# A new order for the steps of a fused attention and expert-layer kernel, behind a fixed beginning

## The chip, the cores and the metric

The kernel runs on one core of one Trainium2 chip. The metric is device time in microseconds of one execution. The kernel before takes 298.82 us, the median of three runs (298.56 to 299.05).

## The reference

The first half is a causal attention with a decay per head and no softmax, over 8 batches of 8 heads, 576 positions and 64 channels; its result, regrouped by position, is the input x (4608 rows of 512) of the second half:

```
scores = scale * np.matmul(q, k.transpose(0, 1, 3, 2))
ret = scores * Dmat          # Dmat = gamma_h ** (i - j) for i >= j, else 0
x = np.matmul(ret, v) ...    # (4608, 512)
h = x @ w_in                 # (4608, 2048)
s = np.sin(alpha * h)
g = h + s * s / (alpha + 1e-09)
out = g @ w_out              # (4608, 512)
```

## The kernel before, in words

The whole work is a list of 1214 small steps, written one to a line in the string TABLE (L18 to L1233). `run` (L1975) splits a line into a name and words and calls the function of that name; nothing reorders the steps afterwards (`tc.manual_schedule()`). So the order of the lines is, engine by engine, the order of the instructions, and each engine takes its own in that order. What one engine needs of another it waits for by semaphore. Words with an @ name the buffer that the step writes (`@raw3`, `@ss1`): a buffer's next writer waits for its last reader. V, A and G name the engine: VectorE, ScalarE, GpSimd (POOL in the profile).

*Blocks.* x is cut into nine blocks of 512 rows. Block b (0 to 7) holds positions 0 to 511 of batch b; block 8 holds the last 64 positions of all eight batches. While TensorE works on the expert layer of block b, the attention of a later batch is made between its matmuls.

*The expert layer.* `project n fc tag` (L1737) is four 512-column matmuls, unit fc (of 16) of block n, into the PSUM bank `tag` (h0, h1, h2, op; m0 and m1 are pairs of banks). `sine` (L1750, ScalarE) reads the bank; `square` (L1758, any engine) squares the sine; `product` (L1767, VectorE) adds the bank to the scaled square and writes g. Only then is the bank free. For blocks 0 to 2, `gemm2 n u tag` (L1780) is four matmuls with w_out and `finish` (L1774) copies 128 finished rows and stores them. From block 3 on the last product is made with seven products of sub-matrices in place of eight: `weight_sum` and `row_sum` (L1814, L1824) make the sums, `part_product` (L1841) is 16 matmuls of 256 columns, and `after_product` (L1875) adds up and stores; `part_product n 7 - first=6` goes on in the bank of product 6, when `after_product n 6` has read it.

*The attention of batch b.* `load` (L1339) brings half p of q, k or v by SyncE's DMA queue into a `raw` buffer; `cast` (L1360) scales it to 16 bits. q and k are transposed on TensorE (`turn`, L1422, then `take`) for batches 0 and 1, later by DMA (`crossed`, L1415, on SyncE's queue too). `at.outer` (L1493) makes the sums of k times v of each 128 positions; `take_sum`, `evict` and `evict_bank` (L1523) copy them out of PSUM; `more` (L1548, two GpSimd instructions) and `next_sum` add them up; `to_state` (L1539) scales the running state. `at.scores` (L1554) and `at.masked` (L1572, VectorE) make the masked scores. `at.values` (L1584) multiplies them with v in two passes (False, then True), and `at.add_states` (L1617) adds the part of the earlier positions. `at.keep` (L1635) copies the result out of PSUM into x: with one engine in one copy, with two in two halves. The first `project` of block b needs both halves p of `at.keep b`. A run of attention matmuls between matmuls of the expert layer is called a stretch.

*Marks.* The second pass of `at.values` may only start when the first is done. With `relay=G` (batches 4 to 7) and in `ends.values` (block 8's attention, L1683) this goes by way of GpSimd: `told` (L1458) puts a no-op into GpSimd's queue that waits for the first pass, and the second pass waits for that no-op:

```
def told(last, eng):
    mark = eng.nop()
    order(mark, last)
    return mark
```

The no-op stands behind all that was put on GpSimd before it. `wait_for_w_out g` (L1918) is a tiny DMA on SyncE's queue that reads a quarter of w_out, so SyncE waits there until that quarter is loaded.

## Time and profile before

| | |
|---|---|
| median of three runs | 298.82 us |
| the profiled execution | 298.66 us |
| its span, first to last instruction | 296.9 us |
| mean granted TensorE clock | 0.989 |
| busy: TensorE, VectorE, ScalarE, GpSimd | 283.9, 234.5, 198.6, 172.6 us |
| `project`: 532 of its matmuls, mean | 372 ns each, overlapping |
| `product` on VectorE | 144 of 743 ns |
| `sine` on ScalarE | 144 of 683 ns |
| `square` on ScalarE, VectorE, GpSimd | 93 of 629, 30 of 510, 21 of 1042 ns |

Matmuls are pipelined, so their pace is read from the starts of two groups and not from the length of one. A row of the timeline gives the start, the length, the engine, the line of the code, the operation, what it writes and reads, and in brackets how long the engine sat idle before it and what ended that. A row of the chain gives start, length and engine with the tile and line. Idle time of an engine other than TensorE costs nothing by itself.

### The profile page before, as it was taken

The numbers are of one execution on the slowest core, as the hardware profiler recorded it, in microseconds if no ns is written. First come the engines' busy times: TensorE is split into PE (matmuls) and PEld (weight loads), VectorE is DVE, ScalarE is ACT, GpSimd is POOL, SyncE is SP. The second block draws the span as 40 slices with busy tenths as digits, with TensorE's granted clock in tenths as the row PEclk, the third lists the DMA queues.
The fourth block names the chain that finished last, engine by engine and source line by source line (L and its number), as shares of the span: only waits on it lengthen the run. The fifth ranks groups of instructions, "written<-read, shape, count | busy, mean of one in ns | idle before, by whom it ended". The sixth has DMA issues, their size and how long they took to land.

```text
span 296.9 us, 8432 instructions
## 1 busy us (share of the span) xinstructions
PE 283.9 (96%) x3480; PEld 182.8 (62%) x3480; DVE 234.5 (79%) x336; ACT 198.6 (67%) x323; POOL 172.6 (58%) x169
## 2 busy tenths in 40 slices
PE   5889999999899999999999999999999999999994
...
GB/s 217 349 230 210 254 293 326 211 196 308 261 237 172 244 171 182 153 253 175 161 240 189 192 140 192 123 199 138 79 55 106 72 4 38 71 0 39 35 107 107
DMA packets 121766, 49.95 MB, mean 168 GB/s; under 512 B 78720, under 2 KB 119680, under 8 KB 121728
## 3 DMA queue, kind: packets, MB, share of 16 engines
...
## 4 chain that ended last, share of the span: by engine, by line
PE 76%; DMA 9%; ACT 5%; DVE 3%; POOL 2%; SPq 2%; issue 2%; ACTq 0%
PE hps L1745 35%; PE hps L1849 23%; PE ops L1785 9%; DMA raw<-in_v_dram 5%; PE sc L1564 2%; PE o L1606 2%; DMA kT<-k 2%; DMA raw<-in_q_dram 2%; SPq L1418 1%; POOL k L1396 1%; ACT v L1320 1%; DVE gT L1769 1%; ACT s L1753 1%; PE kv L1506 1%; DVE xT L1322 1%
## 5 line engine op out<-in xcount | busy, mean ns | idle before, releaser
L1769 DVE SCALAR_TENSOR_TENSOR gT<-ss,inva,hps 128x512 f16<-128x512 f16 x144 | 104.5, 743 | 23.5 <-ACT ss L1762 16.1
L1753 ACT ACTIVATE s<-hps,alpha_t 128x512 f16<-128x512 f32 x144 | 95.8, 683 | 40.5 <-PE hps L1745 31.4
L1745 PE MATMUL hps<-xT,w_in 128*128 128x512 f16 (+1 forms) x532 | 119.3, 372 | 2.1 <-DVE xT L1322 0.9
L1745 PEld LDWEIGHTS <-w_in 128*128 128x128 f16 x596 | 66.1, 114 | 53.1 <-issue 1.6
L1762 ACT ACTIVATE ss<-s 128x512 f16<-128x512 f16 x93 | 58.2, 629 | 7.5 <-DVE gT L1769 5.2
L1764 POOL TENSOR_TENSOR ss<-s 128x512 f16<-128x512 f16 x21 | 21.8, 1042 | 46.7 <-ACT s L1753 34.4
L1785 PE MATMUL ops<-w_out,gT 128*128 128x512 f16 x192 | 45.4, 379 | 0.2 <-DVE gT L1769 0.2
L1396 POOL TENSOR_TENSOR k<-raw,cn 128x1024 f16<-128x1024 f32 (+1 forms) x16 | 26.7, 1676 | 29.3 <-DMA raw<-in_k_dram 29.2
L1849 PEld LDWEIGHTS <-gT 128*128 128x128 f16 x384 | 37.2, 98 | 8.5 <-issue 0.8
L1849 PEld LDWEIGHTS <-S 128*128 128x128 f16 x288 | 28.0, 98 | 5.7
L1785 PEld LDWEIGHTS <-gT 128*128 128x128 f16 x192 | 18.0, 98 | 21.1 <-issue 0.5
L1832 POOL TENSOR_TENSOR S<-gT,S 128x1024 f16<-128x1024 f16 x10 | 22.0, 2207 | 14.7 <-DVE S L1832 10.0
L1551 POOL TENSOR_TENSOR s<-kvs,cn 128x256 f32<-128x256 f32 x21 | 15.4, 735 | 14.0 <-ACT kvs L1320 10.0
L1849 PE MATMUL hps<-T,gT 128*128 128x256 f16 x192 | 22.9, 273 | 0.5 <-DVE mid L1880 0.5
L1764 DVE TENSOR_TENSOR ss<-s 128x512 f16<-128x512 f16 x30 | 15.3, 510 | 9.8 <-ACT s L1753 9.6
L1849 PE MATMUL hps<-w_out,gT 128*128 128x256 f16 x192 | 22.9, 273 | 0.0
L1849 PE MATMUL hps<-w_out,S 128*128 128x256 f16 x192 | 22.9, 273 | 0.0
L1576 DVE TENSOR_TENSOR ret<-sc,mask 128x1024 f16<-128x1024 f32 x16 | 19.2, 1219 | 4.2 <-PE sc L1564 4.2
L1552 POOL TENSOR_TENSOR kvs<-s,kvs 128x256 f32<-128x256 f32 x21 | 17.0, 811 | 2.4 <-DVE kvs L1322 0.9
L1320 ACT CAST xT<-o 128x1024 f16<-128x1024 f32 (+1 forms) x13 | 13.8, 1092 | 6.9 <-PE o L1628 5.2
L1396 POOL TENSOR_TENSOR q<-raw,cn 128x1024 f16<-128x1024 f32 x8 | 15.2, 1904 | 1.5 <-DMA raw<-in_q_dram 1.4
L1396 DVE TENSOR_TENSOR q<-raw,cn 128x1024 f16<-128x1024 f32 (+1 forms) x9 | 12.9, 1440 | 3.7 <-DMA raw<-in_q_dram 3.7
...
## 6 DMA issues: line engine op xcount, KB each, us to landing
...
```

The lines of the kernel that those rows point to most:

```text
L1320: eng.copy(d_, s_)
L1396: eng.tensor_tensor(dst[:, a0:a1].rearrange("p a r t d -> p t (a r) d"), t_.rearrange("p (t a) x -> p t a x", t=2)[:, :, a0:a1].rearrange( ...
L1552: nc.gpsimd.tensor_tensor(self.kvs[:, c], s32, self.kvs[:, c], ADD)
L1576: nc.vector.tensor_tensor(ret.rearrange("p t (z x) -> p (t z) x", z=2)[:, :, 0:n], sc.rearrange("p t (z x) -> p (t z) x", z=2)[:, :, 0:n], ...
L1745: matmul(hps_of[n, fc][0][:, cols], w_in16[fc // 4][:, a, fc % 4 :: 4], xs[n][:, a, cols], start=(a == 0 and part != 1), stop=(a == KT - 1 ...
L1753: nc.scalar.activation(s_t, hps, mybir.ActivationFunctionType.Sin, bias=0.0, scale=alpha_t[:, fc : fc + 1],)
L1762: nc.scalar.activation(ss_t, s_t, mybir.ActivationFunctionType.Square)
L1764: eng.tensor_tensor(ss_t, s_t, s_t, MULT)
L1769: nc.vector.scalar_tensor_tensor(gT[n][:, fc, :], ss_t, inva[:, fc : fc + 1], hps, MULT, ADD)
L1785: matmul(ops[n, c, cols.start][:, cols], gT[n][:, fk, c * P : (c + 1) * P], w_out16[:, fk, cols], start=(fk == 0), stop=(fk == FC - 1), sk ...
L1832: made = eng.tensor_tensor(out_, x, y, op)
L1849: matmul(acc[:, 256 * j : 256 * j + 256], lhs[:, x, 128 * j : 128 * j + 128], rhs[:, x], start=(tag is not None and j == js[0] and p == 0 ...
```

## The change

Only TABLE changes. The first 136 steps stay (up to `product 0 14`, about 33.4 us into the span); of the other 1078 steps, none is added or left out by name, but nearly all stand some places earlier or later, and many have other buffers or banks. 128 of them differ in an engine, a bank or a sub-step order as well:

| step | before | after |
|---|---|---|
| `square` on V, A, G | 30, 93, 21 | 27, 89, 28 |
| `row_sum` on V, G | 31, 17 | 27, 21 |
| `cast` of a whole tile on V, A, G | 11, 8, 36 | 7, 9, 39 |
| `at.evict_bank` on V, A | 6, 4 | 2, 8 |
| `at.take_sum` on V, A | 0, 5 | 2, 3 |

In batch 1, `at.scores 1 0 1` and `at.outer 1 (0)` stood apart and now stand together; in batch 2, `at.outer 2 (0,1)` and `at.scores 2 1 1` stood together and now stand apart. The number of stretches behind the fixed part is 25 in both.

The diff, cut to the places that are spoken of ("..." where lines are left out):

```diff
@@ -152,1083 +152,1083 @@
 at.scores 1 0 0 m1
 load 1 v 0 @raw3
 product 0 14
+load 1 k 1 @raw2
+product 0 10
 project 0 12 h1
 sine 0 12 @s2
-load 1 k 1 @raw4
-product 0 10
-load 1 v 1 @raw2
+square 0 12 A @ss2
+product 0 12
+load 1 v 1 @raw1
 project 0 13 h0
-sine 0 13 @s0
+cast 1 v 0 G @v163
+gemm2 0 4 op
+load 3 k 1 @raw4
 gemm2 0 12 h2
+load 2 k 0 @raw0
+gemm2 0 5 op
...
 at.masked 1 0 0 @ret0
-gemm2 0 4 op
-square 0 13 A @ss3
 at.scores 1 0 1 m0
-square 0 12 G @ss0
...
-cast 1 v 0 A @v162
-gemm2 0 5 op
...
+at.outer 1 (0) h0 h1
...
+at.take_sum 1 1 V @kvs0
+at.take_sum 1 0 V
...
+cast 1 k 1 V @k163
 gemm2 0 13 h2
...
 gemm2 0 14 h2
...
-at.outer 1 (0) h0 h1
-at.take_sum 1 1 A @kvs0
-at.take_sum 1 0 A
...
-cast 1 v 1 A @v161
...
-gemm2 0 6 op
...
-cast 1 k 1 V @k161
...
 gemm2 0 15 h2
...
+cast 1 v 1 A @v160
...
-load 2 q 0 @raw2
+gemm2 0 7 op
+finish 0 3
+wait_for_w_out 1
...
-gemm2 0 7 op
-at.masked 1 1 1 @ret2
...
+gemm2 0 0 h0
 at.masked 1 1 0 @ret3
...
-at.next_sum 1 3
-cast 2 k 0 G @k162
-gemm2 0 0 h0
-load 2 k 1 @raw1
-finish 0 3
-cast 2 q 0 G @q162
-load 2 v 0 @raw5
-gemm2 0 1 h0
-gemm2 0 2 h0
 at.values 1 0 False m1
 at.values 1 0 True
...
+at.add_states 1 0
...
-cast 2 q 1 V @q160
-at.add_states 1 0
-wait_for_w_out 1
...
-at.keep 1 0 V @xT2
+load 2 q 0 @raw3
+at.masked 1 1 1 @ret2
 at.values 1 1 False m0
+at.next_sum 1 3
+at.keep 1 0 V @xT1
 at.values 1 1 True
 at.add_states 1 1
+cast 3 k 1 G @k160
+finish 0 1
+cast 2 k 0 G @k163
+gemm2 0 1 h0
...
 at.keep 1 1 A
-gemm2 0 3 h0
-finish 0 0
-finish 0 1
-project 1 6 m0
...
-load 2 v 1 @raw3
+load 2 k 1 @raw4
+gemm2 0 2 h0
+project 1 6 m1
+load 2 v 0 @raw1
+cast 2 q 0 G @q160
+crossed 2 0 k @kT2
...
+load 2 v 1 @raw0
+cast 2 k 1 G @k162
+cast 2 q 1 V @q162
...
+crossed 2 1 q @qT3
 project 1 8 op
...
-cast 3 k 1 G @k160
...
+gemm2 0 3 h0
+cast 2 v 0 G @v161
...
-cast 2 k 1 G @k161
...
-crossed 2 1 q @qT2
-crossed 2 1 k @kT3
...
-cast 2 v 0 G @v161
...
+cast 2 v 1 G @v160
...
+crossed 2 1 k @kT3
...
-load 3 v 0 @raw2
...
+crossed 2 0 q @qT2
...
+at.outer 2 (0,1) m1
+load 3 k 0 @raw3
...
-cast 2 v 1 G @v160
-at.outer 2 (0,1) m1
...
+gemm2 0 8 h0
...
-crossed 2 0 q @qT3
-crossed 2 0 k @kT1
...
+gemm2 0 9 h0
...
 at.scores 2 1 1 m0
-load 3 k 0 @raw0
...
-gemm2 0 8 h0
-gemm2 0 9 h0
...
-load 3 v 1 @raw3
...
+load 3 v 1 @raw5
...
+load 3 v 0 @raw4
+gemm2 0 10 h0
...
-load 3 q 0 @raw4
...
-at.scores 2 0 0 m0
...
-gemm2 0 10 h0
...
+at.scores 2 0 0 m0
...
 at.add_states 2 0
 at.add_states 2 1
+cast 3 v 0 G (0) @v162
+cast 3 v 0 G (1)
+cast 3 k 0 G @k162
 at.outer 3 (0,1) op h2
-cast 4 v 0 G @v160
+at.keep 2 0 V A @xT0
+at.keep 2 1 A V
+gemm2 1 6 h0
+load 4 v 0 @raw5
+square 1 15 G @ss2
+product 1 15
+crossed 3 1 k @kT0
+at.evict_bank 3 1 A @kvs0
+project 2 7 m1
+at.evict_bank 3 0 A
...
+gemm2 1 12 h1
...
+gemm2 1 13 h1
...
+gemm2 1 7 h0
...
+gemm2 1 14 h1
...
+gemm2 1 15 h1
...
+gemm2 1 8 h0
...
-at.keep 2 0 V A @xT1
-at.evict_bank 3 1 A @kvs0
-at.evict_bank 3 0 V
...
-gemm2 1 6 h0
-gemm2 1 7 h0
-at.keep 2 1 A V
-project 2 7 m1
...
+project 2 14 h2
+at.evict_bank 4 0 A @kvs0
...
+project 2 8 op
 at.masked 3 0 1 @ret0
...
-project 2 14 h2
...
-at.masked 3 0 0 @ret2
-project 2 8 op
...
-at.evict_bank 4 0 V @kvs0
+at.values 3 0 False m0
+at.values 3 0 True
+at.add_states 3 0
 at.values 3 1 False m1
 at.values 3 1 True
...
+at.add_states 3 1
+at.keep 3 0 A V @xT2
+at.keep 3 1 A
...
+at.evict_bank 4 1 V
+product 2 14
+project 2 10 h0
...
+project 2 11 h1
...
+project 2 15 m1
...
-at.values 3 0 False m0
-at.values 3 0 True
-at.evict_bank 4 1 V
...
-at.add_states 3 0
...
-at.add_states 3 1
...
-at.keep 3 0 A V @xT0
...
-product 2 14
-at.keep 3 1 V
...
-project 2 10 h0
...
-project 2 11 h1
...
-project 2 5 h2
...
-project 2 12 m0
-project 2 15 m1
...
+row_sum 3 S4 1 G told_to=G
...
+cast 6 k 0 G @k161
...
+at.more 5 2 @s320
...
-cast 6 k 0 G @k161
...
 cast 6 q 0 G @q162
...
-row_sum 3 S4 1 V told_to=G
...
+at.to_state 5 1 G
...
+cast 6 v 1 G @v161
...
+at.to_state 5 2 G
...
+square 4 8 G @ss3
+at.more 5 3 @s320
 cast 6 k 1 G @k163
...
-at.to_state 5 0 @s160
...
-square 4 8 G @ss1
...
+row_sum 4 S3 0 G
...
+at.to_state 5 3
...
+at.values 5 0 False m0 relay=G
...
-at.to_state 5 3
-at.to_state 5 1 G
...
-at.to_state 5 2 G
...
-row_sum 4 S3 0 G
 at.values 5 1 False m1 relay=G
...
+square 5 6 G @ss3
...
-at.to_state 6 3
-row_sum 4 S4 1 G told_to=G
...
-square 5 6 A @ss0
...
-at.to_state 6 2
-cast 7 k 0 G @k161
+row_sum 4 S4 1 G told_to=G
...
-cast 7 k 1 G @k163
...
-row_sum 5 S3 0 G
...
 cast 4 k 2 G
...
+cast 7 k 1 G @k163
+cast 7 v 1 G @v163
...
+at.more 6 3 @s321
...
+at.to_state 6 0 @s161
...
+at.to_state 6 2
...
+cast 7 v 0 V @v162
...
+cast 2 q 2 G
...
+cast 7 q 1 G @q160
...
-cast 2 q 2 G
-cast 7 q 0 G @q160
...
+row_sum 5 S3 0 G
...
+at.to_state 6 1
+at.values 6 1 False m1 relay=G
...
 at.values 6 0 False m0 relay=G
-at.values 6 1 False m1 relay=G
...
-product 7 2
...
 ends.masked 0
...
+square 7 3 A @ss1
...
+product 7 3
+product 7 2
...
-square 7 3 V @ss1
-product 7 3
...
+ends.masked 2
...
-ends.masked 2
...
 part_product 6 6 op
...
+after_product 6 6
...
-after_product 6 6
...
+part_product 6 7 - first=6
...
-part_product 6 7 - first=6
...
-part_product 8 6 h0
...
+part_product 8 1 op
+row_sum 8 S2 0 G
+part_product 8 6 h2
...
+part_product 8 2 h0
...
+part_product 8 7 - first=6
...
+row_sum 8 S1 1 G
 row_sum 8 S4 1 V
...
-part_product 8 2 h1
-part_product 8 7 - first=6
-row_sum 8 S1 0 V
...
-row_sum 8 S1 1 G
-row_sum 8 S4 0 V
-part_product 8 5 op
...
+row_sum 8 S1 0 G
+part_product 8 5 h1
...
-part_product 8 4 m0
+part_product 8 4 m1
+row_sum 8 S4 0 G
+part_product 8 3 h1 (0)
...
-part_product 8 3 h2 (0)
+part_product 8 3 m0 (1)
...
-part_product 8 3 h1 (1)
```

More of the change, by code (lines that the diff above doesn't have):

```diff
@@ new lines @@
+project 2 15 m1
+sine 2 15 @s2
+product 2 11
+square 2 10 A @ss0
+product 2 10
+crossed 4 1 q @qT3
+project 2 5 h2
+sine 2 5 @s0
+project 2 12 m0
+sine 2 12 @s3
+square 2 12 G @ss1
+cast 0 k 2 G
+square 2 15 V @ss2
+load 5 q 1 @raw2
+square 2 5 V @ss0
+product 2 5
+gemm2 2 0 op
+project 3 1 h1
+load 1 q 2
+project 3 0 h0
+at.more 4 1 @s321
+at.to_state 4 1 G
+cast 5 v 0 A @v162
+product 2 12
+load 5 k 1 @raw5
+sine 3 1 @s2
+project 3 2 h2
+product 2 15
+sine 3 0 @s3
+square 3 0 A @ss3
+square 3 1 V @ss2
@@ new lines @@
+sine 3 10 @s3
+square 3 10 A @ss2
+project 3 8 h1
+crossed 0 2 k
+cast 5 k 0 G @k162
+at.masked 4 0 1 @ret2
+load 2 k 2
+project 3 12 m0
+project 3 11 h2
+load 2 q 2
+gemm2 2 8 op
+crossed 5 0 k @kT3
+gemm2 2 9 op
+sine 3 12 @s3
+gemm2 2 10 op
+gemm2 2 11 op
+crossed 5 1 k @kT2
+sine 3 11 @s2
+square 3 11 G @ss1
+product 3 10
+square 3 12 A @ss3
+product 3 12
+at.to_state 4 3 G
+at.to_state 4 2 A
+cast 5 v 1 A @v163
+product 3 11
+finish 2 2
+at.values 4 1 False m1 relay=G
+at.outer 5 (0,1) h0 h2
@@ new lines @@
+part_product 3 2 - first=1
+at.more 5 2 @s320
+sine 4 7 @s2
+square 4 7 A @ss1
+sine 4 3 @s0
+square 4 3 A @ss2
+project 4 1 h0
+project 4 4 h1
+load 6 q 1 @raw4
+load 4 k 2
+product 4 7
+product 4 3
+after_product 3 2
+load 3 k 2
+sine 4 1 @s1
+square 4 1 A @ss3
+at.scores 5 0 0 m1
+at.masked 5 0 0 @ret3
+at.scores 5 0 1 m0
+load 5 k 2
+part_product 3 6 op
+sine 4 4 @s0
+square 4 4 A @ss0
+project 4 8 m1
+cast 6 q 0 G @q162
+project 4 6 h2
+sine 4 6 @s1
+product 4 1
+product 4 4
+square 4 6 A @ss0
@@ L742 @@
-after_product 3 3
-at.evict_bank 6 1 V
-at.more 6 1 @s321
-crossed 6 0 k @kT2
-cast 6 q 1 V @q160
+square 4 12 A @ss2
+after_product 3 5
+project 4 11 h1
+sine 4 11 @s2
+square 4 11 A @ss1
+part_product 3 3 - first=5
+at.masked 5 1 1 @ret0
+product 4 12
+at.values 5 0 False m0 relay=G
+product 4 10
+at.outer 6 (0,1) h0 h2
+at.masked 5 1 0 @ret1
+at.values 5 1 False m1 relay=G
 at.values 5 0 True
 at.add_states 5 0
+at.values 5 1 True
+crossed 6 0 k @kT2
+crossed 6 0 q @qT2
+at.add_states 5 1
 at.keep 5 0 A @xT0
-row_sum 4 S4 0 G
```

1422 lines of the change are left out of this document (658 added, 764 removed).

## The prediction

> **What bounds the kernel now.** I read the page first (engine totals and the row of 40 slices), then the chain that ended last, then the timeline of TensorE alone around every gap, then VectorE, ScalarE, GpSimd and SyncE around the same moments.
>
> ```profile
> span 296.9 us, 8432 instructions
> PE 283.9 (96%) x3480; PEld 182.8 (62%) x3480; DVE 234.5 (79%) x336; ACT 198.6 (67%) x323; POOL 172.6 (58%) x169
> PE   5889999999899999999999999999999999999994
> ```
>
> TensorE is busy 96% of the span, and both kernels give it the same 3480 matmuls. So the change can win only time in which TensorE stands idle behind the first step that moves, and it can lose by making new idle time. The chain gives the pitch of the matmuls when nothing waits:
>
> ```profile
> 83.65 3.45 PE ops L1785 x16
> 142.47 1.75 PE hps L1849 x16
> 117.64 0.47 PE sc L1564 x32
> 67.13 0.97 PE ops L1785 x4
> 68.10 0.86 PE hps L1745 x4
> 33.48 9.96 DMA raw<-in_v_dram
> 43.47 1.05 ACT v L1320
> 61.22 5.45 DMA kT<-k
> ```
>
> Sixteen 512-column matmuls take 3.45 us: 0.216 each, 0.86 for a `project` or a `gemm2`, 1.75 for a `part_product`. A group behind attention matmuls takes 0.97 instead of 0.86, so leaving a stretch of attention costs 0.11. Against that pitch, TensorE's timeline has six gaps behind the step at which the tables part (near 33.4 us); the bracket is the idle time and its releaser:
>
> ```profile
> 33.66 1.67 PE L1745 MATMUL hps<-xT,w_in 128*128 128x512 f16 x7
> 35.51 1.46 PE L1785 MATMUL ops<-w_out,gT 128*128 128x512 f16 x6 [0.17 <-DVE gT L1769]
> 50.43 1.04 PE L1785 MATMUL ops<-w_out,gT 128*128 128x512 f16 x4
> 51.90 1.46 PE L1745 MATMUL hps<-xT,w_in 128*128 128x512 f16 x6 [0.43 <-ACT xT L1320]
> 64.64 1.46 PE L1745 MATMUL hps<-xT,w_in 128*128 128x512 f16 x6
> 66.72 0.42 PE L1564 MATMUL sc<-qT,kT 64*64 64x128 f16 x16 [0.61 <-DMA kT<-k]
> 76.38 1.90 PE L1785 MATMUL ops<-w_out,gT 128*128 128x512 f16 x8
> 79.15 1.05 PE L1745 MATMUL hps<-xT,w_in 128*128 128x512 f16 x4 [0.87 <-DVE xT L1322]
> 102.97 1.92 PE L1745 MATMUL hps<-xT,w_in 128*128 128x512 f16 x8
> 105.39 0.81 PE L1745 MATMUL hps<-xT,w_in 128*128 128x512 f16 x3 [0.50 <-DVE gT L1769]
> 238.13 1.46 PE L1745 MATMUL hps<-xT,w_in 128*128 128x512 f16 x6
> 240.13 0.60 PE L1849 MATMUL hps<-T,gT 128*128 128x256 f16 x4 [0.55 <-DVE mid L1880]
> ```
>
> From start to start, less the matmuls between at 0.216: 0.34, 0.61, 0.78, 1.04, 0.69 and 0.70 us, together 4.2 us. Everything else behind 33 us is back to back. That 4.2 us (1.4%) is all that a reordering of these steps can win; each gap is therefore followed into the new order.
>
> **The change part by part.** By name the two tables hold the same 1214 steps, and TensorE's sum at the pitch above is the same. Batch 1 has one stretch of attention less (`at.scores 1 0 1` and `at.outer 1 (0)` now join), but batch 2 has one more (`at.outer 2` and `at.scores 2 1 1` now stand apart), so the 0.11 is won and spent: zero. What is left is waiting.
>
> *Gap at 35.5 (0.34).* `gemm2 0 12` waited for bank h2, which `product 0 14` still read. `gemm2 0 4` now comes first and covers it. But in both orders `at.outer 1 (1)` stands behind the same matmuls and needs `cast 1 v 1`, which began at 43.47, when its load had landed. That load is third on SyncE in both. So up to 44.5 us nothing is won: 0.
>
> *Gap at 51.9 (0.61).* The first `project` of block 1 waited for ScalarE's copy of x (`at.keep 1 1`), with one `gemm2` (0.86) as cover. Now two stand between (`gemm2 0 1`, `gemm2 0 2`; `gemm2 0 3` follows later): −0.61. If that cover were short again, the 0.61 would stay.
>
> *Gap at 66.7 (0.78).* `at.scores 2 0 0` waited for `crossed 2 0 k`, the fourth of the four transposes on SyncE's queue, landed 5.45 us after its issue at 61.22. In the new order that one is first and `crossed 2 0 q` last, `load 3 v 0` has gone behind all four, and TensorE asks later by `gemm2 0 10`, which now stands ahead, and a stretch more: 66.72 − 0.78 − 0.61 + 0.86 + 0.2 = 66.4. The last transposition must then be issued by 66.4 − 5.45 = 60.9, where the old one was issued at 61.22 with a load more ahead of it: −0.78. SyncE also meets `wait_for_w_out 1` three steps sooner, ahead of `load 2 q 0` and all that follows:
>
> ```profile
> L1920 SPq DMA_DIRECT2D zero<-w_out x2: 896/1060/1224, 48.5 to 128.1; - x2
> ```
>
> It waits for nothing, since `gemm2 0 5` reads that quarter of the weights before it in both orders, but its issue holds the queue for about 1.1 us, which the loads behind it lose and the earlier place of the transposes gives back. The price of it all: `cast 3 k 1` now stands ahead of `cast 2 k 0` on GpSimd and frees raw4 for `load 2 k 1`, so `cast 2 k 1`, `cast 2 v 0` and `cast 2 v 1` come out of GpSimd close to when `at.outer 2` and `at.scores 2 1 1` ask for them. The trace of before has no such wait; I bound it by 0 and by a wait like the largest here, 1.0, and take +0.3, nearer to the smallest gap (0.34).
>
> *Gap at 79.15 (1.04).* The rows of the two copying engines:
>
> ```profile
> 75.73 0.74 DVE L1322 CAST xT<-o 128x512 f16<-128x512 f32 x1
> 76.50 0.74 ACT L1320 CAST xT<-o 128x512 f16<-128x512 f32 x1 [1.63 <-DVE xT L1322]
> 76.57 0.69 DVE L1322 COPY kvs<-kv 128x512 f32<-128x512 f32 x1
> 77.10 0.58 ACT L1320 COPY kvs<-kv 128x512 f32<-128x512 f32 x1
> 77.57 0.75 ACT L1320 CAST xT<-o 128x512 f16<-128x512 f32 x1
> 78.35 0.74 DVE L1322 CAST xT<-o 128x512 f16<-128x512 f32 x1 [1.09 <-ACT xT L1320]
> ```
>
> The two halves of one `at.keep` do not run side by side: ScalarE waits for VectorE, then VectorE for ScalarE, four copies in a row. The new order takes the `kvs` copy out of the middle (77.57 − 77.10 = 0.47 sooner, x ready at about 78.65) but also takes `gemm2 1 7` out of the cover: `project 2 7` is due at 76.38 + 0.86 = 77.24. The wait is about 1.43 instead of 1.04: +0.39. (With `gemm2 1 7` back as cover it would be 0.57.)
>
> *Gap at 105.4 (0.69).* `project 2 5` waited for bank h2, because `product 2 14` stood behind a copy of x on VectorE. Now `at.keep 3 1` is ScalarE's, and values of half 0 come first. But `at.evict_bank 4 1` (0.69 on VectorE) stands behind the second half of `at.keep 3 0`, and it must free h1 for `project 2 11`, one `project` after the attention ends at E. The copy chain starts about 0.95 before E (two groups of 16 matmuls at 0.42, by the row at 66.72, and the states): 0.74 + 0.74 + 0.69 − 0.95 = 1.2 against a cover of 0.86. A new wait of 0.4 for 0.69: −0.3.
>
> *Gap at 240.1 (0.70).* VectorE came late with `after_product 6 6`. The cause is seven us earlier:
>
> ```profile
> 232.91 2.13 POOL L1832 TENSOR_TENSOR S<-gT 128x1024 f16<-128x1024 f16 x1
> 233.46 1.86 DVE L1764 TENSOR_TENSOR ss<-s 128x512 f16<-128x512 f16 x1
> ```
>
> The square of unit 3 took 1.86 us on VectorE, and ended 0.3 behind GpSimd's row sum. Such a square is VectorE's quickest operation elsewhere in the trace, so 1.4 us went to waiting on GpSimd. `square 7 3` is now ScalarE's and `ends.masked 2` stands behind two products: −0.70.
>
> *GpSimd's new work.* Squares go from 21 to 28 there and row sums from 17 to 21; VectorE gives up three of the squares and the four row sums, ScalarE four squares. That costs nothing while GpSimd reaches its marks in time: with `relay=G`, the second half of `at.values` waits for a no-op in GpSimd's queue, behind everything put there before.
>
> ```profile
> 185.53 1.04 POOL L1764 TENSOR_TENSOR ss<-s 128x512 f16<-128x512 f16 x1 [0.92 <-DVE gT L1769]
> 186.52 2.13 POOL L1832 TENSOR_TENSOR gT<-gT 128x1024 f16<-128x1024 f16 x1
> 188.60 1.05 POOL L1380 TENSOR_TENSOR ks<-ks,cn 128x512 f16<-128x512 f32 x1
> 190.60 1.91 POOL L1396 TENSOR_TENSOR q<-raw,cn 128x1024 f16<-128x1024 f32 x1
> 156.86 1.18 POOL L1544 TENSOR_TENSOR s<-kvs,cn 128x256 f16<-128x256 f32 x2
> 55.89 1.03 POOL L1322 CAST v<-raw 128x1024 f16<-128x1024 f32 x1
> ```
>
> and the page's groups for the two halves of an `at.more`:
>
> ```profile
> L1551 POOL TENSOR_TENSOR s<-kvs,cn 128x256 f32<-128x256 f32 x21 | 15.4, 735 | 14.0 <-ACT kvs L1320 10.0
> L1552 POOL TENSOR_TENSOR kvs<-s,kvs 128x256 f32<-128x256 f32 x21 | 17.0, 811 | 2.4 <-DVE kvs L1322 0.9
> ```
>
> From `square 5 6` to the mark of batch 6 the new queue holds one square 1.04, two row sums 4.26, two small casts 2.10, two large casts 3.82, one cast of v 1.03, one `at.more` 1.55 and three states 1.77: 15.6 us without a pause. TensorE from the end of `project 5 6` to the second half has ten `project`s 8.6, four `part_product`s 7.0, scores 0.5 and about 1.0 of values and outer products: 17.1, less about 0.7 for the sine that the square waits for. Slack 0.8 us. Batch 5 has a like chain, from `row_sum 3 S4 1` (2.13 + 1.91 + 1.55 + 1.91 + 0.59 + 1.03 + 0.59 + 1.04 + 1.55 + 1.91 + 2.13 + 0.59 = 16.9) against a cover that VectorE's speed decides. I take +0.3 for both, between 0 and the price of rival 3.
>
> *The rest.* The other moved steps (sines, products, loads two or more places ahead of their use) lie beside TensorE's dense work; a bank is asked for again no sooner than 2.6 us of matmuls after its `project`, against 2.5 before. At the end `row_sum 8 S4 0` moves to GpSimd: two sums of S1 (4.3) under three `part_product`s (5.25), then 2.13 under two more (3.5), so nothing, unless GpSimd starts over 1 us late. A thousand steps in new places will hide one wait that I don't see; I add one of the smallest size found above, +0.3.
>
> Sum: −0.61 − 0.78 + 0.3 + 0.39 − 0.3 − 0.70 + 0.3 + 0.3 = −1.1 us. The profiled execution took 298.66 us (span 296.9 and 1.76 around it), the median of the runs is 298.82, 0.16 more: 298.82 − 1.1 = 297.7.
>
> **The rivals.** 1, *all covers hold*: the terms that I added for GpSimd, transposes and the unseen wait are zero: −2.0, 296.8; without the new wait at h1 also 296.4. For it: the gaps of before are short and lie all at the change of a block. Against: two of the new margins come out under 0.5 us.
>
> 2, *nothing is won*: the transposes and casts of batch 2 take the full 1.0, `project 2 7` waits 1.43, and one more wait like the 0.7 at 240 appears where VectorE shares with GpSimd: −1.1 + 0.7 + 0.7 = +0.3, 299.1. For it: transfers differ much from one to the next (9.96 us from issue to landing for one load in the chain, 5.45 for a transposition), and GpSimd has more to do.
>
> 3, *slower: GpSimd late at the marks of batches 5 and 6*. If each instruction of these chains lasts 15% longer, each is 2.4 us longer, and TensorE waits 2.4 − 0.8 = 1.6 at batch 6 and up to 2.4 at batch 5: 4.0 in place of the 0.3, 301.4. It turns the result to slower by over 0.6 us once the two waits pass 2.0 us together (−1.1 − 0.3 + 2.0 = 0.6), that is from chains about 9% longer. For it: GpSimd and VectorE held each other up at 233. Against: by the row at 190.60 GpSimd was busy up to 192.51 in the old order too, right at batch 6's mark, and TensorE's timeline has no gap there. The Trainium skill (SBUF — State Buffer, section "SBUF: two separate sides") says that the port pair these two engines share is an exclusive lock held for a whole instruction, whichever engine comes first. The square of 1.86 us agrees for VectorE; by that rule GpSimd is blocked just as fully, the chains grow, and the time would be rival 3's.
>
> **How the numbers follow.** About 0.2% (0.6 us) is what a measurement here can tell from no change: faster is below 298.2, slower above 299.4. The forecast has 0.5, with an own range of 297.1 to 298.4, nearly all of it faster; rival 1 has 0.12, rival 2 0.22, rival 3 0.16. Faster: 0.46 + 0.12 = 0.58; same: 0.04 + 0.2 = 0.24; slower: 0.16 + 0.02 = 0.18. The range runs from rival 1's lower end, 296.3, to 299.8, which leaves out most of rival 3 and little else.
>
> **What would show it.** Right: no wait of TensorE for a copy of x before block 1, none for a transposed k, none for `mid`; about 1.4 us for x before block 2 and 0.4 for `kvs` before `project 2 11`; TensorE's busy time unchanged. Wrong: a wait of the second half of `at.values` in batch 5 or 6 with GpSimd busy right before it, a wait of `at.outer 2` for a cast, or several waits of VectorE's products.

## The result, and the profile after

The changed kernel takes 297.12 us (median of 20 runs, 296.60 to 298.84); the kernel before took 298.94 in the same comparison (298.00 to 304.72). The ratio is 0.9943, 95% interval 0.9928 to 0.9958: 0.57% or 1.8 us faster. The prediction said 297.7 (296.3 to 299.8) and put 0.58 on faster. Ratios, here and below, leave out the few runs that lie more than 1.5% above the fastest of their kernel.

The profiled execution of the changed kernel took 297.88 us (span 296.2), that of the kernel before 298.66 (span 296.9). So the two profiles stand 0.78 us apart and the medians 1.82. The 1.04 between the two has two parts: the profiled execution of before lay 0.28 under the median of its kernel, that of the changed kernel 0.76 over its own. Page of the changed kernel: span, TensorE's total, TensorE's 40 slices.

```profile
span 296.2 us, 8430 instructions
...
PE 283.9 (96%) x3480; PEld 182.8 (62%) x3480; DVE 222.6 (75%) x320; ACT 198.9 (67%) x324; POOL 196.2 (66%) x184
...
PE   6789999999899999999999999999999999999994
```

TensorE's busy time is the same to the tenth; VectorE has 12 us less to do, GpSimd 24 more. What changed for TensorE is idle time alone. TensorE's timeline of the changed kernel at the places that the prediction named (start, length, engine and line, tiles, count; idle time and releaser in brackets):

```profile
48.63 1.90 PE L1785 MATMUL ops<-w_out,gT 128*128 128x512 f16 x8
50.37 1.89 PE L1745 MATMUL hps<-xT,w_in 128*128 128x512 f16 x8
...
65.58 1.03 PE L1745 MATMUL hps<-xT,w_in 128*128 128x512 f16 x4
66.53 0.42 PE L1564 MATMUL sc<-qT,kT 64*64 64x128 f16 x16
...
75.38 1.04 PE L1785 MATMUL ops<-w_out,gT 128*128 128x512 f16 x4
77.62 1.67 PE L1745 MATMUL hps<-xT,w_in 128*128 128x512 f16 x7 [1.20 <-DVE xT L1322]
...
97.64 0.72 PE L1506 MATMUL kv<-v,k 64*64 64x64 f16 x64
98.87 0.42 PE L1564 MATMUL sc<-qT,kT 64*64 64x128 f16 x16 [0.51 <-DVE gT L1769]
...
103.00 1.05 PE L1745 MATMUL hps<-xT,w_in 128*128 128x512 f16 x4
104.29 1.89 PE L1745 MATMUL hps<-xT,w_in 128*128 128x512 f16 x8 [0.24 <-DVE kvs L1322]
...
239.27 1.91 PE L1849 MATMUL hps<-T,gT 128*128 128x256 f16 x16
```

Three waits of before are gone: block 1's first `project` (50.37), the scores of batch 2 (66.53) and `part_product 6 7` (239.27). The wait for x before `project 2 7` grew to 1.37 start to start, and 0.43 for `kvs` is new before `project 2 11`; both were forecast. Not named was 0.69 before `at.scores 3 0 1`. In front of 45 us stand 0.32 and 0.29 for the last inputs of batch 1 (before: 0.18 at the second of these places, and the 0.34 at 35.5). These five waits sum to 3.1 us, where the six gaps of before had 4.2. TensorE's last matmul ends at 292.30, before at 293.10; so of 1.1 to 1.3 us less waiting 0.8 arrives there. The rest lies in the spacing of the other matmuls, and no row singles it out.

Two things are left to explain: the 0.69, and how much of a closed gap is kept, since one profile shows one execution.

### The profile page after: what moved, and what is told of

It is laid out like the page before. It is cut to its first block, busy times and chain, and to the rows that moved or that the text cites. A ratio compares the mean times of both kernels' runs of the same rounds, so it can differ in the third digit from the quotient of the medians.

```text
span 296.2 us, 8430 instructions
## 1 busy us (share of the span) xinstructions
PE 283.9 (96%) x3480; PEld 182.8 (62%) x3480; DVE 222.6 (75%) x320; ACT 198.9 (67%) x324; POOL 196.2 (66%) x184
## 4 chain that ended last, share of the span: by engine, by line
PE 81%; DMA 9%; DVE 3%; POOL 2%; ACT 2%; issue 1%; SPq 1%; POOLq 0%; ACTq 0%
PE hps L1745 39%; PE hps L1849 25%; PE ops L1785 10%; DMA raw<-in_v_dram 3%; DMA w_in<-in_moe_w_in_dram 3%; PE o L1606 2%; DMA raw<-in_k_dram 2%; PE sc L1564 2%; PE kv L1506 1%; SPq L1350 1%; POOL ss L1764 1%; DVE xT L1322 1%; ACT s L1753 1%; PE o L1628 1%; DVE ss L1764 1%
## 5 line engine op out<-in xcount | busy, mean ns | idle before, releaser
L1753 ACT ACTIVATE s<-hps,alpha_t 128x512 f16<-128x512 f32 x144 | 97.2, 686 | 45.9 <-PE hps L1745 41.9
L1745 PE MATMUL hps<-xT,w_in 128*128 128x512 f16 (+1 forms) x532 | 120.8, 372 | 2.0 <-DVE xT L1322 1.2
L1762 ACT ACTIVATE ss<-s 128x512 f16<-128x512 f16 x89 | 55.5, 631 | 4.3 <-DVE gT L1769 2.2
L1764 POOL TENSOR_TENSOR ss<-s 128x512 f16<-128x512 f16 x28 | 29.0, 1042 | 43.3 <-ACT s L1753 27.9
L1396 POOL TENSOR_TENSOR k<-raw,cn 128x1024 f16<-128x1024 f32 (+1 forms) x17 | 28.5, 1687 | 6.7 <-DMA raw<-in_k_dram 6.2
L1832 POOL TENSOR_TENSOR S<-gT,S 128x1024 f16<-128x1024 f16 x9 | 19.8, 2210 | 10.3 <-DVE S L1832 10.3
L1396 POOL TENSOR_TENSOR q<-raw,cn 128x1024 f16<-128x1024 f32 x12 | 23.1, 1925 | 4.9 <-DMA raw<-in_q_dram 3.4
L1320 ACT CAST xT<-o 128x1024 f16<-128x1024 f32 (+1 forms) x14 | 15.4, 1114 | 6.3 <-PE o L1628 4.0
L1551 POOL TENSOR_TENSOR s<-kvs,cn 128x256 f32<-128x256 f32 x21 | 14.5, 692 | 6.5 <-PE o L1628 2.9
L1576 DVE TENSOR_TENSOR ret<-sc,mask_halved 128x768 f16<-128x768 f32 x16 | 14.9, 947 | 1.9 <-PE sc L1564 1.9
```

Source lines behind the costliest of these rows:

```text
L1320: eng.copy(d_, s_)
L1396: eng.tensor_tensor(dst[:, a0:a1].rearrange("p a r t d -> p t (a r) d"), t_.rearrange("p (t a) x -> p t a x", t=2)[:, :, a0:a1].rearrange( ...
L1576: nc.vector.tensor_tensor(ret.rearrange("p t (z x) -> p (t z) x", z=2)[:, :, 0:n], sc.rearrange("p t (z x) -> p (t z) x", z=2)[:, :, 0:n], ...
L1745: matmul(hps_of[n, fc][0][:, cols], w_in16[fc // 4][:, a, fc % 4 :: 4], xs[n][:, a, cols], start=(a == 0 and part != 1), stop=(a == KT - 1 ...
L1753: nc.scalar.activation(s_t, hps, mybir.ActivationFunctionType.Sin, bias=0.0, scale=alpha_t[:, fc : fc + 1],)
L1762: nc.scalar.activation(ss_t, s_t, mybir.ActivationFunctionType.Square)
```

## First experiments: three gaps closed one at a time in the kernel before

Theory A: the gaps of the profiled execution are all that an order can win, and a gap closed is won. Rivals: the wait is handed on to the next step (B), or the gain lies elsewhere (C). Each part of the change was put into the kernel before by itself.

**b_cover**

```diff
 gemm2 0 1 h0
-gemm2 0 2 h0
...
 at.keep 1 1 A
+gemm2 0 2 h0
 gemm2 0 3 h0
```

> The kernel before with one step moved: gemm2 0 2 stands behind at.keep 1 1, next to gemm2 0 3, so 1.72 us of matmuls and not 0.86 lie between the attention of batch 1 and the first project of block 1. Theory A (TensorE's gaps behind 33 us are the whole of what the order can win, and a gap closed is won): the wait of project 1 6 for ScalarE's copy of x (0.43 idle, 0.61 start to start) goes, nothing else changes, and the time falls by 0.6 us, to 298.3 where before takes 298.9. Rival B (TensorE is held to SyncE's queue, which is issuing without a pause from 52 to 68 us, so a wait closed early is handed on): project 1 6 does not wait, but the wait for the transposed k before at.scores 2 0 0 grows from 0.78 to about 1.3 us, and the time stays within 0.2 of before.

Measured: 299.26 us beside 299.27, ratio 0.9990 (0.9966 to 1.0014), which by itself does not exclude the 0.6. The wait before `project 1 6` is gone, as both theories said. Its profiled execution took 300.25, 1.0 over the median (in 11 of the 13 kernels that were run besides before, the profiled execution lay over the median of the runs), and shows three other waits: two are new, and the one for x before `project 2 7` has grown from 1.04 to 1.56. The wait at 66.7, which rival B expected to grow, is 0.60. The rows of TensorE, ScalarE and SyncE (SPq is the time that an issue holds the queue):

```profile
54.12 3.09 SPq L1418 DMA_TRANSPOSE qT<-q  x1
...
61.32 0.42 PE L1564 MATMUL sc<-qT,kT 64*64 64x128 f16 x16 [0.42 <-DMA kT<-k]
...
73.23 1.04 ACT L1320 CAST v<-raw 128x1024 f16<-128x1024 f32 x1 [2.90 <-DMA raw<-in_v_dram]
...
76.95 0.70 PE L1506 MATMUL kv<-v,k 64*64 64x64 f16 x64 [1.16 <-DVE gT L1769]
...
80.88 1.49 PE L1745 MATMUL hps<-xT,w_in 128*128 128x512 f16 x6 [1.40 <-DVE xT L1322]
```

The same rows of the kernel before:

```profile
54.49 1.40 SPq L1418 DMA_TRANSPOSE qT<-q  x1
...
72.00 1.05 ACT L1320 CAST v<-raw 128x1024 f16<-128x1024 f32 x1 [1.55 <-DMA raw<-in_v_dram]
```

One and the same transposition held SyncE for 1.40 us in one execution and 3.09 in the other. In the second, `crossed 2 1 k` behind it came late for TensorE (0.78 from start to start). This first wait is more than chance: in all four profiles with this edit (b_cover and, below, b_three, b_four and b_five) TensorE is ready for `at.scores 2 1 1` at 60.5 to 60.7 and starts it at 61.17 to 61.44, where before started it at 61.26 without a wait, and in b_three the transposition ahead held the queue for only 1.41. So the 0.6 won at 51.9 is handed on to `crossed 2 1 k`. Further on, `load 3 v 1` fed `cast 3 v 1` at 73.23 and not at 72.00. That cast is ScalarE's and stands ahead of `sine 1 12`; ScalarE sat 2.90 us before it, the sine, square and product of unit 12 followed late, and the outer products of batch 3 waited 1.33 us for the bank (1.67 from 75.28, the start of the matmuls ahead, where before has 0.34). In the kernel before the same cast was waited for as well, by ScalarE alone: it had just enough room.

**b_gemm**

```diff
+gemm2 0 10 h0
 at.scores 2 0 0 m0
...
-gemm2 0 10 h0
```

> The kernel before with one step moved: gemm2 0 10 (0.86 us of matmuls) stands ahead of at.scores 2 0 0 instead of behind it. Theory A: the scores are asked for at 66.80 where the transposed k landed at 66.67, so the wait of 0.78 us goes and the time falls by 0.8, to 298.1. Rival B (handed on): the wait at 66.7 goes, and one of the same size comes up later in block 1 or at the change to block 2, where x is late for project 2 7 (1.04 us there now); the time stays within 0.2 of before.

Measured: 299.45, ratio 1.0005 (0.9983 to 1.0027). The scores of batch 2 wait no more. A wait of 1.41 us has come up 33 us later, in the outer products of batch 4, for GpSimd's `cast 4 k 1` (2.06 from their start to the next `project`, 0.65 before):

```profile
99.76 0.45 PE L1506 MATMUL kv<-v,k 64*64 64x64 f16 x32 [1.26 <-POOL k L1396]
...
91.14 1.05 POOL L1396 TENSOR_TENSOR k<-raw,cn 128x512 f16<-128x512 f32 x1 [9.88 <-DMA raw<-in_k_dram]
...
97.81 1.90 POOL L1396 TENSOR_TENSOR k<-raw,cn 128x1024 f16<-128x1024 f32 x1
...
81.44 1.23 DVE L1396 TENSOR_TENSOR q<-raw,cn 128x1024 f16<-128x1024 f32 x1 [2.26 <-DMA raw<-in_q_dram]
```

GpSimd sat idle for 9.88 us before `cast 4 k 0`, until SyncE's `load 4 k 0` had landed, and from there to the end of `cast 4 k 1` it was busy throughout. In the kernel before the same chain began at 89.64 and ended at 98.20, and TensorE asked for it at 98.54: 0.34 us of room. Here SyncE issued that load at 84.73 and not at 83.24, and TensorE came 0.46 sooner. The last row shows why: ahead of the load SyncE had to issue `crossed 3 1 q` (82.70, 81.22 before), which waited for VectorE's `cast 3 q 1`, and that for `load 3 q 1`. This load took 6.77 us from issue to landing, 4.30 in the kernel before. In b_four, b_five, b_keep and b_late it took 6.2 to 6.7, in b_square 4.34. With the chain of before, which ended at 98.20, TensorE would have come 0.1 us too early, so nearly all of the 1.41 is this slow transfer. Whether the edit made it slow, no run shows; b_late, which closes no gap, has it too.

**b_square**

```diff
-square 7 3 V @ss1
+square 7 3 A @ss1
```

> The kernel before with one word changed: square 7 3 is done by ScalarE and not by VectorE. Theory A with the lock (VectorE's 16-bit square cannot run beside GpSimd's instruction, 1.86 us in place of about 0.42): VectorE comes to after_product 6 6 about 1.8 us sooner, TensorE's wait for mid at 240.1 (0.70 us) goes, and the time falls by 0.7, to 298.2. Rival (only the 0.42 us of work counts, the rest is an artefact of the profile or would hit the next instruction of VectorE instead): VectorE is 0.4 sooner, about 0.3 us of the wait stays, and the time falls by 0.4 or less.

Measured: 298.46, ratio 0.9986 (0.9957 to 1.0014), too wide to tell the two theories apart. The profile is clear: TensorE's matmuls around `part_product 6 7` are back to back,

```profile
237.74 1.89 PE L1745 MATMUL hps<-xT,w_in 128*128 128x512 f16 x8
239.46 1.80 PE L1849 MATMUL hps<-T,gT 128*128 128x256 f16 x15
```

the last matmul ends at 292.42, 0.68 before that of the kernel before, and the profiled execution is 0.68 shorter (297.98). The whole 0.70 went, not 0.4: the square's whole 1.86 us had counted. It was also kept, and behind 240 us there is no late load for it to be handed on to.

**b_three**, all three edits.

> The kernel before with the three edits together: gemm2 0 2 behind at.keep 1 1, gemm2 0 10 ahead of at.scores 2 0 0, square 7 3 on ScalarE. Theory A: 0.61 + 0.78 + 0.70 = 2.1 us less, of which up to 0.5 comes back at the transposed k, since TensorE now asks for it 0.6 sooner and SyncE does not issue it sooner: 296.8 to 297.4, the whole of what the change measured (1.8 less). Rival C (the change's gain comes from elsewhere: VectorE's lighter load over the whole kernel, 222.6 us busy against 234.5, or waits that this one profile of before does not show): three edits of four lines win 0.8 or less, 298.1 or more.

Measured: 298.90, ratio 0.9988 (0.9968 to 1.0008). Theory A falls: 2.1 us of gaps closed won at most 1.0. Its profile has the waits of b_cover again, 0.78 before `at.scores 2 1 1`, 1.34 before the outer products of batch 3 and 1.54 before `project 2 7`, and no gap at 240.

## Second experiments: SyncE's queue

Theory D, formed on these rows: from 44 to about 120 us the kernel before is tied to what SyncE feeds it, whose issues and transfers differ in length from execution to execution, and TensorE coming earlier meets the next late feed. (In the prediction SyncE's queue bore on the transposes of batch 2 alone.)

**b_four**

```diff
 load 3 k 0 @raw0
+load 3 v 1 @raw3
...
 load 4 v 0 @raw5
...
-load 3 v 1 @raw3
```

and the edits of b_three.

> The kernel before with the three edits of the first set and one load moved: load 3 v 1 stands right behind load 3 k 0 on SyncE, ahead of load 4 v 0 and of the rest of block 1's loads. Theory D (from 44 to 85 us SyncE issues its DMAs without a pause, and their lengths differ by chance from execution to execution, the same transposition taking 1.4 or 3.1 us; a wait that is closed earlier is handed on to the next step that needs SyncE late; in the kernel before that is cast 3 v 1, which stands ahead of the sine of unit 12 in ScalarE's queue and was fed at 73.2 and 73.6 us where TensorE had come early): load 3 v 1 is issued about 3.5 us sooner, cast 3 v 1 waits no more, the 1.45 us that TensorE waited before the outer products of batch 3 go, the wait before project 2 7 falls from 1.5 to about 1.0, and the time is 1.0 to 2.0 below that of the three edits, 297.0 to 297.9 where before takes 299.2. Theory C (the gain of the change lies elsewhere): 298.5 or more.

Measured: 298.29, ratio 0.9959 (0.9938 to 0.9980), 1.2 us faster than before and by the ratios about 0.9 better than b_three, where 1.0 to 2.0 was expected; the intervals of the two overlap, so the 0.9 is not shown by the times alone. TensorE's timeline:

```profile
75.28 0.71 PE L1506 MATMUL kv<-v,k 64*64 64x64 f16 x64
...
78.69 1.49 PE L1745 MATMUL hps<-xT,w_in 128*128 128x512 f16 x6 [0.86 <-DVE xT L1322]
...
99.65 0.45 PE L1506 MATMUL kv<-v,k 64*64 64x64 f16 x32 [1.13 <-POOL k L1396]
```

The outer products of batch 3 wait no more and the wait for x is back at 1.03, as theory D said; the next late feed, `cast 4 k 1` again, takes 1.29 us (the expectation of b_five has 1.40).

**b_keep** is the edit of a_keep (below), which won 1.4 us in the changed kernel, made in the kernel before.

```diff
-at.keep 2 0 V A @xT1
+at.keep 2 0 V @xT1
+at.keep 2 1 A
...
-at.keep 2 1 A V
```

> The kernel before with the same edit that won 1.3 us in the changed kernel: batch 2's copies of x out of PSUM whole, half 0 by VectorE and half 1 by ScalarE, here with the second put ahead of the two copies of kvs. Theory D: project 2 7 starts without its 1.04 us of waiting, but cast 4 k 1, which hangs on SyncE's loads and not on TensorE, ended at 98.20 with TensorE asking at 98.54; of the 1.0 won at 79 us, 0.7 comes back before project 2 14, and the time falls by 0.3, to 299.1 where before takes 299.4. Theory A: the whole 1.0 is kept, 298.4.

Measured: 299.32, ratio 0.9992 (0.9962 to 1.0021), with runs from 296.73 to 303.55.

```profile
78.29 1.03 PE L1745 MATMUL hps<-xT,w_in 128*128 128x512 f16 x4
...
99.76 0.45 PE L1506 MATMUL kv<-v,k 64*64 64x64 f16 x32 [1.42 <-POOL k L1396]
```

`project 2 7` does not wait, and the outer products of batch 4 wait 1.59 us in its place, more than the 0.7 expected, since the chain of casts came later here too (`cast 4 k 1` from 97.81, behind a `load 3 q 1` of 6.55 us). By the medians the same edit is worth 1.4 us in one order (0.6 to 2.2) and 0.2 in the other (−0.6 to 1.1). The intervals overlap; it is the traces that show where the gain went, to a feed that hangs on SyncE's queue and on a transfer.

**b_five** mends that feed too.

```diff
-load 0 v 2
 crossed 3 1 q @qT1
+load 4 k 0 @raw1
+load 0 v 2
 load 4 q 0 @raw5
-load 4 k 0 @raw1
...
+load 4 k 1 @raw0
 crossed 3 0 k @kT1
...
-load 4 k 1 @raw0
...
-make_mask_halved
...
 cast 4 q 0 G @q161
+make_mask_halved
```

and the edits of b_four.

> The kernel before with the edits of b_four and the feed of cast 4 k 1 put earlier as well: load 4 k 0 ahead of load 0 v 2 and load 4 q 0, load 4 k 1 ahead of crossed 3 0 k, make_mask_halved on GpSimd behind cast 4 q 0. In b_four GpSimd sat 9.6 us before cast 4 k 0 because load 4 k 0 came late from SyncE, everything behind it followed, and TensorE waited 1.40 us before project 2 14 for cast 4 k 1. Theory D (waits are handed on along SyncE's late queue until the last late feed is mended): cast 4 k 1 begins at 95 to 96 and not at 97.7, the 1.40 goes, no wait of its size takes its place behind 100 us, and the time is about that of the change, 297.0 to 297.8 where before takes 299.4. Theory C (the change's gain needs its thousand other moves): 298.2 or more.

Measured: 298.78, ratio 0.9994 (0.9968 to 1.0020). The expectation fell in its second half. `cast 4 k 1` ends at 98.67, and TensorE does not wait for it; but it waits twice for transposes that this order has put later (the second was issued at 116.12, before at 112.62):

```profile
98.76 0.64 PE L1564 MATMUL sc<-qT,kT 64*64 64x128 f16 x32 [0.96 <-DMA qT<-q]
...
119.98 0.37 PE L1564 MATMUL sc<-qT,kT 64*64 64x128 f16 x16 [1.37 <-DMA kT<-k]
```

Moving a load forward moves others back, and in the kernel before several feeds up to batch 4 have little room. Room here is the time from a transposition's landing (or a cast's end) to the step of TensorE that needs it, from the trace; a dash where the landing isn't in the trace:

| feed | before | b_square | after | a_late |
|---|---|---|---|---|
| `crossed 2 0 k` | 0.04 (waited) | 0.04 (waited) | – | 10.55 |
| `crossed 2 1 q` | 1.50 | 1.63 | 4.50 | – |
| `crossed 3 0 q` | 2.10 | – | 6.24 | 3.08 |
| `cast 4 k 1` | 0.34 | 0.87 | 2.81 | 0.48 |
| `crossed 4 1 k` | 1.53 | 2.07 | 4.99 | 5.35 |

The transposes have 3 us or more in the changed order. `cast 4 k 1` is still close there: 0.48 in a_late, and in a_keep (below) it ends 0.23 ahead of the outer products, no more than in the kernel before. So what the change did beside closing gaps was to put the transposes ahead of their use. That this is why its closed gaps are kept is likely by the table, but no run takes that room away from the changed order.

**b_late and a_late** asked for the same thing from the other side: SyncE made later, in both kernels.

b_late:

```diff
+wait_for_w_out 0
 crossed 2 0 q @qT3
...
+wait_for_w_out 0
 load 3 v 1 @raw3
```

> The kernel before with two needless tiny DMAs more on SyncE's queue, reads of a quarter of w_out that is loaded long before, at 59 and 67.7 us, ahead of crossed 2 0 q and of load 3 v 1; each holds the queue for 0.5 to 1.4 us by the issues of this kind in the profiles. Theory D: the queue is behind in the kernel before, so the transposed k comes about 1 us later (the wait at 66.7 grows from 0.78 to about 1.8) and load 3 v 1 up to 2 us later, which holds ScalarE and through it the outer products of batch 3; the time rises by 1.0 to 2.0, to 300.2 to 301.2. Theory A (only the gaps of the profiled execution count, SyncE is not the bound): the time rises by 0.3 or less.

a_late:

```diff
+wait_for_w_out 0
 load 3 k 0 @raw3
...
+wait_for_w_out 0
 load 3 q 1 @raw0
```

> The changed kernel with the same two needless tiny DMAs on SyncE's queue at the same times, 59.7 and 68 us, ahead of load 3 k 0 and of load 3 q 1. Theory D: the change has put the transposes of batch 2 and the loads of batch 3 so far ahead of their use (load 3 v 1 issued at 61.1 where it was 67.7, its cast on GpSimd) that 1 to 2 us more are absorbed: no wait of TensorE for a copy or cast of batch 3 before 79 us, and the time rises by 0.3 or less, to 297.4 at most. Rival (the change only shifted the waits, it is no more tolerant of SyncE than the kernel before): it rises by 1.0 or more, like the kernel before.

Measured: b_late 299.97, ratio 1.0018 (0.9994 to 1.0041); a_late 297.96, ratio 0.9956 (0.9938 to 0.9975), where the changed kernel has 0.9943. In time they tell nothing apart: +0.5 us (−0.2 to +1.2) and +0.4, both inside the intervals, and the 1.0 to 2.0 that theory D expected of b_late is not there. The added issues were short, 0.52 and 0.63 us in b_late, 0.54 and 1.04 in a_late. Nor does b_late's profile show the waits that were expected: the one at 66.7 fell from 0.78 to 0.3, and the outer products of batch 3 waited 0.3. It has others: the wait for x before `project 2 7` grew to 1.64, and two more are in these rows. b_late:

```profile
56.09 2.90 SPq L1420 DMA_TRANSPOSE kT<-k  x1
...
59.73 0.52 SPq L1922 DMA_DIRECT2D zero<-w_out  x1
...
61.70 0.42 PE L1566 MATMUL sc<-qT,kT 64*64 64x128 f16 x16 [0.50 <-DMA kT<-k]
...
100.82 0.45 PE L1508 MATMUL kv<-v,k 64*64 64x64 f16 x32 [0.93 <-POOL k L1398]
```

The wait at 61.70 owes nothing to the added DMAs: the transposition that it waits for was issued ahead of them, and held the queue for 2.90 us. It is a late feed by chance, which the one profile of the kernel before does not have. The wait at 100.82 is `cast 4 k 1` again, which b_gemm, b_four and b_keep had without added DMAs. So b_late does not test theory D. a_late has no wait for a transposition or a cast of batches 2 to 4. Its last matmul ends at 292.27, the changed kernel's at 292.30, but that they agree is luck: a_late started the outer products of batch 1 0.67 later (45.16) and had no 0.69 at 98 us.

## Third experiments: what the changed kernel still waits for

**a_keep**

```diff
-at.keep 2 0 V A @xT0
-at.keep 2 1 A V
+at.keep 2 0 V @xT0
+at.keep 2 1 A
```

> The changed kernel with batch 2's copies of x out of PSUM made in one piece each, half 0 by VectorE and half 1 by ScalarE, in place of two pieces each by both. The prediction took the order of the four pieces (0.74 us each, one after the other) as given. Theory: two engines on one pair of banks take turns, two engines on two pairs do not, as batch 1's whole copies (1.33 and 1.31 us, overlapping by 0.4) show; x is ready at about 76.2 and not at 77.6, project 2 7 follows gemm2 1 6 with no wait or one of 0.1, 1.37 us of waiting go, and the time falls by 1.2, to 295.9. Rival (copies by ScalarE and VectorE out of PSUM never run side by side): x is ready at 74.7 + 1.33 + 1.31 = 77.4, and nothing is won.

Measured: 296.06, ratio 0.9897 (0.9877 to 0.9918), 1.4 us below the changed kernel's 0.9943. The two copies now overlap, and `project 2 7` follows its `gemm2`:

```profile
74.36 1.32 DVE L1322 CAST xT<-o 128x1024 f16<-128x1024 f32 x1 [1.05 <-PE o L1628]
...
74.58 1.34 ACT L1320 CAST xT<-o 128x1024 f16<-128x1024 f32 x1 [1.74 <-PE o L1628]
...
75.07 1.04 PE L1785 MATMUL ops<-w_out,gT 128*128 128x512 f16 x4
75.97 1.30 PE L1745 MATMUL hps<-xT,w_in 128*128 128x512 f16 x5
```

Four halves of 0.74 in a row took 2.9 us in the changed kernel; two wholes of 1.33 side by side are done 1.6 us after the first began.

**a_all**

```diff
-at.keep 2 0 V A @xT0
-at.keep 2 1 A V
+at.keep 2 0 V @xT0
+at.keep 2 1 A
...
-square 2 4 V @ss2
+square 2 4 A @ss2
...
+at.evict_bank 4 1 V
 at.keep 3 0 A V @xT2
 at.keep 3 1 A
...
-at.evict_bank 4 1 V
```

> The changed kernel with the whole copies of x of batch 2, with square 2 4 on ScalarE, and with at.evict_bank 4 1 ahead of at.keep 3 0. Theory (each of TensorE's waits in the changed kernel has a local cause and SyncE is no longer late): the wait for x before project 2 7 goes (1.37), the one for kvs before project 2 11 goes (0.43), and the one before at.scores 3 0 1, for a square that ran 2.01 us beside GpSimd's cast in one of three profiles of this order, cannot come (0.69 at most, 0.2 in the mean); the time is 0.4 to 0.7 below the whole copies alone, 295.4 to 295.7. Rival (the waits are handed on here too): 296.0 or more.

Measured: 295.53 (295.35 to 295.81), ratio 0.9881 (0.9868 to 0.9895): 3.6 us under the kernel before and the lowest median here. Its profile has no wait of TensorE above 0.3 us behind 76 us, so the waits were not handed on. From 101.29 on its timeline has one run of matmuls where the changed kernel waited for `kvs`:

```profile
101.29 3.00 PE L1745 MATMUL hps<-xT,w_in 128*128 128x512 f16 x13
```

The three edits were not each run alone. The first is a_keep; what the other two add, 0.5 by the ratios, lies inside the intervals.

The square is there for the 0.69. In four profiles of this order `square 2 4` meets GpSimd's casts at different moments. The changed kernel, then a_late, then a_keep (a_mark, below, is the fourth):

```profile
91.93 2.90 POOL L1396 TENSOR_TENSOR k<-raw,cn 128x512 f16<-128x512 f32 x2
...
93.10 2.01 DVE L1764 TENSOR_TENSOR ss<-s 128x512 f16<-128x512 f16 x1 [1.39 <-ACT s L1753]
```

```profile
93.78 4.09 POOL L1398 TENSOR_TENSOR k<-raw,cn 128x512 f16<-128x512 f32 x3
...
93.81 1.30 DVE L1766 TENSOR_TENSOR ss<-s 128x512 f16<-128x512 f16 x1 [1.39 <-ACT s L1755]
```

```profile
89.87 1.91 POOL L1396 TENSOR_TENSOR q<-raw,cn 128x1024 f16<-128x1024 f32 x1
...
91.51 0.54 DVE L1764 TENSOR_TENSOR ss<-s 128x512 f16<-128x512 f16 x1 [1.39 <-ACT s L1753]
```

The square lasts 2.01, 1.30 and 0.54 us (0.72 in a_mark), and each time it ends 0.27 or 0.28 behind the end of a GpSimd cast: the cast that ends at 94.83 (91.93 + 2.90), the first of a_late's three at 94.83, the one that ends at 91.78. Only in the first did TensorE wait for `product 2 13`. In a_late the square ended at the same 95.11, but TensorE, late since 45 us, came to the scores at 98.10 and not at 97.39. So the 0.69 depends on when both engines come there, and a square on VectorE is safe only where GpSimd is known to rest.

**a_mark**

```diff
+cast 7 q 0 G @q162
 row_sum 5 S3 0 G
...
 at.to_state 6 1
 at.values 6 1 False m1 relay=G
...
-cast 7 q 0 G @q162
```

> The changed kernel with cast 7 q 0 (1.90 us on GpSimd) ahead of row_sum 5 S3 0, and so ahead of the mark of batch 6; nothing else is moved and no engine does more. In the profile GpSimd came to that mark 0.26 us before TensorE was done with the first pass. Theory (rival 3 of the prediction names a real mechanism, with a margin of 0.26 us in place of the 0.8 that it reckoned): TensorE waits 1.6 us before the second pass of at.values 6, and the time rises by 1.6, to 298.7. Rival (TensorE's queue holds other work to fill it, or the wait is made up behind): 0.3 or less, 297.4.

Measured: 297.88, ratio 0.9963 (0.9950 to 0.9976), 0.6 us over the changed kernel's 0.9943, with intervals that overlap; what follows rests on the trace. Neither theory holds. TensorE and GpSimd around the mark:

```profile
193.00 0.36 PE L1606 MATMUL o<-ret,v 64*64 64x128 f16 x16
...
194.49 0.42 PE L1628 MATMUL o<-qT,s 64*64 64x128 f16 x16 [0.71 <-POOL s L1544]
...
191.74 2.13 POOL L1832 TENSOR_TENSOR gT<-gT 128x1024 f16<-128x1024 f16 x1
193.83 0.61 POOL L1544 TENSOR_TENSOR s<-kvs,cn 128x256 f16<-128x256 f32 x1
```

The second pass starts at 193.00, while GpSimd is in a row sum that ends at 193.87 and has `to_state 6 1` still to do. Both stand ahead of the no-op in its queue. So a mark does not wait for the work ahead of it to be done. What TensorE waits for, 0.71 us, is the state itself, which `at.add_states 6 1` reads: it is ready at 194.44, and was at 192.88 in the changed kernel, 1.03 us ahead of its use.

## Why the prediction was right, point by point

*Gaps at 51.9, 66.7 and 240.* All three went, with the sizes given. Their causes held too, but the steps that took −0.61 and −0.78 as won because the cover is there are only half the reason: b_cover and b_gemm have the same covers and their profiles show the gain lost again. b_cover's 0.6 went to `crossed 2 1 k`, b_gemm's 0.8 to `cast 4 k 1` and the slow load ahead of it. That they are kept in the changed order is put down here to the loads and transposes that it also moved; that is argued from the table of room and not shown by a run of its own.

*+0.3 for the casts of batch 2.* Zero: `at.outer 2` and `at.scores 2 1 1` did not wait.

*Gap at 79.* 1.37 measured, 1.43 forecast. Right as a sum, and blind in its premise: it took the four copies in turn as given, when the whole copies of batch 1 stood in the same trace.

*Gap at 35.5 and `kvs` before `project 2 11`.* The outer products of batch 1 start at 44.49 (44.57 before), the forecast 0; and 0.43 against 0.4.

*+0.3 for GpSimd's marks, and rival 3.* Zero, and by the wrong mechanism. The step that failed is "behind everything put there before": a_mark shows that the mark passes. The chain itself came out as forecast: from `square 5 6` to the end of `to_state 6 1` GpSimd took 15.8 us (177.05 to 192.88), where 15.6 was reckoned and rival 3 needed chains 9% longer. The Trainium skill (Perfetto Trace Analysis, section "Per-engine timelines") describes instructions that the sequencer carries out by itself and others that it hands to an engine's queue, free for the next at once. If the no-op is of the first kind, it passes work still running, and a_mark agrees, by 0.87 us (193.87 − 193.00). The price of lateness on GpSimd is that of the states.

*The lock in rival 3.* The Trainium skill (SBUF — State Buffer, section "SBUF: two separate sides") has either engine blocked by the other. For VectorE the squares agree, 2.01 us against 0.42. For GpSimd two rows of the kernel before agree:

```profile
79.57 1.62 DVE L1396 TENSOR_TENSOR q<-raw,cn 128x1024 f16<-128x1024 f32 x1
...
80.19 1.59 POOL L1552 TENSOR_TENSOR kvs<-s,kvs 128x256 f32<-128x256 f32 x1
```

GpSimd's addition takes 1.59 beside VectorE's cast and ends 0.59 behind it, as in b_square; in b_gemm, where the two do not meet, it takes 0.73 and the cast 1.23. So GpSimd is held up too, but at the marks the two engines met too little for it to matter: the chain of batch 6 was 0.2 us longer than reckoned, and TensorE waited at neither mark.

*+0.3 for an unseen wait.* It was the 0.69 in the profiled execution, and nothing in the three other profiles of this order.

*The size.* −1.1 was forecast, −1.8 measured between the medians. The terms that came out otherwise are the three allowances of +0.3: without them the sum is −2.0, which is rival 1's. By this arithmetic the direction was right for the gaps named, and the size was off by what was added for safety. The two profiles stand only 0.78 apart because the changed kernel's profiled execution lay 0.76 over its median; a_keep's profile has neither its 0.69 nor its 0.29 in front of 45 us, so executions without them exist, but how often they come, no run shows.

*"That 4.2 us is all that a reordering of these steps can win."* No run won more: a_all won 3.6. What fails is the working behind it, that a gap closed is a gap won: b_three closed 2.1 us of gaps and won 0.4 (at most 1.0). The profile of one execution shows only the late feeds of that execution. b_late shows one more by chance, and b_cover, b_gemm, b_keep, b_four and b_five show how near the others lie. The spread of the runs fits: half of the 20 of the kernel before lie within 298.6 and 300.0, half of the changed kernel's within 297.0 and 297.6. Rival 2 named this chance ("transfers differ much from one to the next") and placed it in the changed kernel; the runs show more of it in the kernel before.
